# Batch 1's q transposed on TensorE instead of by DMA, and batch 2's loads requested ahead of the last w_out chunk

## The chip, the cores and the metric

The kernel runs on one core of a Trainium2 chip. A core has five engines with an instruction queue each: TensorE (PE, matrix products; its weight loads are listed apart as PEld), VectorE (DVE), ScalarE (ACT), GpSimd (POOL) and SyncE (SP, which here only requests transfers). Transfers are carried by 16 DMA engines; those that SP requests go through a queue that the profile calls q1, those that POOL requests through q0. The metric is the device time of one execution in microseconds (us); less is better. The kernel before took 294.74 us, the median of 3 runs (294.08 to 295.0).

## The reference: what is computed

An attention without a score matrix, followed by a two-layer block with a sine in it:

```
q_s = softmax of q over its 64 channels          # q, k, v: (8 batches, 8 heads, 576, 64), float32
k_s = softmax of k over its 576 positions
kv  = k_s^T v                                    # per batch and head, 64 x 64
x   = q_s kv, heads side by side                 # 4608 tokens x 512
h   = x @ w_in                                   # 512 -> 2048
g   = h + sin(alpha * h)^2 / (alpha + 1e-9)
out = g @ w_out                                  # 2048 -> 512, float32
```

## The kernel before, in words

Products are in bf16, sums in float32. Tokens are handled in 9 tiles of 512 for the two-layer block and in 8 batches of 576 for the attention, so a tile of the block needs one or two batches. The transposed attention output `xT`, `w_in` and `w_out` stay in on-chip memory. `w_out` comes in four chunks of 4 x 128 rows by `load_wout` (L110), requested by POOL because they are cast from float32 to bf16 on the way. q, k and v of a batch come by `load` (L94 in two halves, L96 in one piece), requested by SP into a pool of five staging buffers; `load_batch` requests all three.

The attention of a batch has these steps. `exp_q` and `exp_k` (ACT, L117) take exponentials. `norm_q` sums over the channels on DVE (L144, L145) and multiplies on POOL for the first half of the heads and on DVE for the second (L146), giving `qn`. `cast_v` (L131) makes v bf16 with a column of ones. q has to be transposed: `q_transpose_dma` (L196) does that by DMA from SP, `q_transpose` (L179 to L181) by products with an identity on PE into PSUM and a copy out. `kv_mm` (L157) forms the kv products and `kv_norm` (L167, L170) divides by the sums and writes `kbd`. `attn_chunk` (L214) multiplies `kbd` with transposed q, and a copy (L419 for batch 1) writes `xT`.

The order of the instructions on each engine is the order in which the program lists them; no scheduler changes it. Each engine takes its list in order and waits by semaphores. The products of one tile with `w_out` are a generator, and `take(os, n)` places the next n of them. For tile 0 that is `o_quad`: 64 products in four groups of 16, group c reading only chunk c of `w_out`. So the products from the 49th on need the fourth chunk, which `load_wout(3)` requests.

The stage at hand lies between tile 0 and tile 1 of the block. In it batch 1's attention is made, while the first 48 of the 64 products of tile 0 with `w_out` run on PE: 20, a short piece of attention for batch 0, then 26, then 2, then the kv products of batch 1, then 4 products, an attention pair for the first half of the heads, 2, the pair for the second half, 2 and the rest. Copies of the four finished sums (L260) and their stores (L263, eight of them on SP) follow. Tile 1's first products (L234) come next. PSUM tiles of this stage come from `ps_e`, two buffers with the tag "a" that are handed out in turn: `tp` of `q_transpose`, `kvp` of `kv_mm` and `xp` of the attention share them. The accumulators of `o_quad` are the four buffers of `ps_h`, which tile 1's products take over.

In the order written out, SP has, after v of batch 1: the two transposes of q of batch 1, the loads of batch 2, the eight stores, the loads of q and k of batch 3. POOL has `norm_q`'s first half and then the request of the fourth `w_out` chunk.

Of the kernel before, what the change touches and what calls it, by code (L numbers as in the profile page):

```python
# [23 lines left out]
def kernel(  # L24
# [51 lines left out]
    def src_view(t, b):  # L76
        return t[b].rearrange("(i e) (p j) d -> (e p) i (j d)", e=2, j=J)
# [7 lines left out]
    def load(name, t, b, halves=False, eng=nc.sync, gate=None):  # L85

        st = stage.tile([128, 4, J, D], F32, name=f"st_{name}", tag="st")
        for ii in range(2) if gate else ():
            gate(st[:, ii, 0, 0:1], zero)
        view = src_view(t, b)  # L90
        flat = st.rearrange("p i j d -> p i (j d)")
        if halves:
            for ii in range(2):
                eng.dma_start(out=flat[:, ii::2], in_=view[:, ii::2])  # L94
        else:
            eng.dma_start(out=flat, in_=view)  # L96
        staged[name, b] = st

    def load_batch(b):
        load("q", q, b)  # L100
        load("k", k, b)
        load("v", v, b)
# [6 lines left out]
    def load_wout(c):  # L109
        nc.gpsimd.dma_start(out=wout[:, 4 * c:4 * c + 4, :], in_=wout_v[:, 4 * c:4 * c + 4, :])  # L110
# [9 lines left out]
    def exp_q(b):  # L120
        A["qe", b] = att2.tile([128, J, 4 * D], BF16, name="qe")
        exp_to(A["qe", b], staged["q", b])

    def exp_k(b):
        A["ke", b] = att2.tile([128, J, 4 * D], BF16, name="ke")
        exp_to(A["ke", b], staged["k", b])

    def cast_v(b, engs):
        vv = vb[b % 2].rearrange("p j (i c) -> p i j c", i=4)
        for ii in range(2):  # L130
            engs[ii](vv[:, 2 * ii:2 * ii + 2, :, 0:D], staged["v", b][:, ii::2])  # L131

    def norm_q(b, engs):

        qe = A["qe", b].rearrange("p j (ii x d) -> p ii j x d", ii=2, x=2)
        A["qn", b] = qn = att1.tile([128, 2, J, 2 * D], BF16, name="qn")
        qs = small.tile([128, J, 4], F32, name="qs")
        if len(engs) == 1:
            nc.vector.tensor_reduce(qs, A["qe", b].rearrange("p j (i d) -> p j i d", i=4), axis=AXL.X, op=ALU.add)  # L139
            nc.vector.reciprocal(qs, qs)  # L140
        for ii in range(2):
            part = qs[:, :, 2 * ii:2 * ii + 2]
            if len(engs) == 2:
                nc.vector.tensor_reduce(part, qe[:, ii], axis=AXL.X, op=ALU.add)  # L144
                nc.vector.reciprocal(part, part)  # L145
            engs[ii % len(engs)].tensor_tensor(qn[:, ii].rearrange("p j (x d) -> p j x d", x=2), qe[:, ii],  # L146
                                               part.unsqueeze(3).to_broadcast([128, J, 2, D]), op=ALU.mult)
# [25 lines left out]
    def q_tile(b):  # L173
        if ("qT", b) not in A:
            A["qT", b] = att2.tile([128, 2, J, 128], BF16, name="qT")
        return A["qT", b]

    def q_transpose(b, ii, pool, eng):
        tp = pool.tile([128, 16, 128], BF16, name="tp", tag="a")  # L179
        q_transpose_ii(b, ii, 0, J, tp)  # L180
        eng(q_tile(b)[:, ii], tp[:, 0:J])  # L181

    def q_transpose_ii(b, ii, j0, j1, tp):

        for j in range(j0, j1):
            nc.tensor.transpose(tp[:, j - j0], A["qn", b][:, ii, j], identb)

    def q_transpose_dma(b, halves=False):
        for ii in range(2) if halves else (slice(0, 2),):
            out, in_ = q_tile(b)[:, ii], A["qn", b][:, ii]  # L190
            if not halves:
                out, in_ = out.rearrange("p ii j c -> p (ii j) c"), in_.rearrange("p ii j c -> p ii (j c)")
                in_ = in_.rearrange("p ii c -> p (ii c)")
            else:
                in_ = in_.rearrange("p j c -> p (j c)")
            nc.sync.dma_start(out=out, in_=in_, transpose=True)  # L196
# [14 lines left out]
    def attn_chunk(b, c, j0, j1, xp):  # L211

        ii, e = divmod(c, 2)
        nc.tensor.matmul(xp, kbd[b % 2][:, e, ii], A["qT", b][:, ii, j0:j1, e * 64:(e + 1) * 64],  # L214
                         start=True, stop=True)
# [6 lines left out]
    def mm_h(t, ni, wide=None, k0=0, k1=4):  # L222

        if ni == 0 and k0 == 0:
            G[t] = gpool.tile([128, nN, MF], BF16, name="g")
        if k0:
            hp = HP[t, ni]
        elif wide and ni % 6 in ((2, 3) if t == 0 else (4, 5)):
            hp = wide()
        else:  # L230
            hp = ps_h.tile([128, MF], F32, name="hp", tag="h")
        HP[t, ni] = hp
        for ki in range(k0, k1):
            nc.tensor.matmul(hp, win[:, ki, ni * 128:(ni + 1) * 128],  # L234
                             xT[:, ki, t * MF:(t + 1) * MF], start=(ki == 0), stop=(ki == 3))
        return hp
# [30 lines left out]
    ACT_CP, DVE_CP, GP_CP = nc.scalar.copy, nc.vector.tensor_copy, nc.gpsimd.tensor_copy  # L267
# [23 lines left out]
    ps_e = ES.enter_context(tc.tile_pool(name="ps_e", bufs=2, space=PSUM, reuse_waits="tile"))  # L291
# [54 lines left out]
    def h_slot(t, ni, sq, lag, wide=None):  # L346
        hp = mm_h(t, ni, wide, 2 if t < 2 and ni < 2 else 0)
        lag.append((t, ni, hp, sine(t, ni, hp, sq)))

    def flush(lag, keep):  # L350
        while len(lag) > keep:
            combine(*lag.pop(0))

    def o_quad(t, accs, engs):

        R = range(4)
        orders = [[(n, m) for p in (0, 2) for n in R for m in (p, p + 1)],
                  [(n, m) for n in R for m in R], [(n, m) for n in R for m in R],
                  [(n, m) for m in R for n in R]]
        for c in R:  # L360
            for n, m in orders[c]:
                mm_o(t, m, 4 * c + n, accs[m])
                if c == 3 and n == 3:
                    evac_o(t, m, accs[m], engs[m])
                yield

    def take(it, n=1000):
        for _ in range(n):
            if next(it, 0) == 0:
                return  # L370
# [4 lines left out]
    with ES:  # L375
        def lent():
            return ps_e.tile([128, 2, MF], F32, name="hh", tag="a")[:, 0]

        late = {6: lambda: load("q", q, 1, halves=True, gate=DVE_CP), 8: lambda: load_wout(2),
                13: lambda: load("k", k, 1, halves=True, gate=DVE_CP)}  # L380
        for ki in range(2):
            for ni in range(2):
                mm_h(0, ni, lent, ki, ki + 1)
        for ni in range(nN):
            h_slot(0, ni, "DPAPPAPPAPPAPPAP"[ni], lag, lent)
            flush(lag, 1)
            if ni in late:
                late[ni]()
        flush(lag, 0)

        accs = [ps_h.tile([128, dm], F32, name="hp", tag="h") for _ in range(4)]
        os = o_quad(0, accs, [DVE_CP, ACT_CP, DVE_CP, ACT_CP])
        take(os, 20)
        xp = ps_e.tile([128, 4, P], F32, name="xp", tag="a")
        for c in range(4):
            attn_chunk(0, c, 8, 9, xp[:, c])
        DVE_CP(xT[:, :, 8 * P:9 * P], xp)
        take(os, 26)
        exp_q(1)
        load("v", v, 1, halves=True)  # L400
        norm_q(1, [GP, V])
        load_wout(3)
        exp_k(1)
        cast_v(1, [ACT_CP, DVE_CP])
        q_transpose_dma(1, halves=True)
        load_batch(2)
        nc.scalar.activation(zero, zero, AX.Sin)
        take(os, 2)
        for ii in range(2):
            kv_mm(1, ii, ps_e, split=True)  # L410
            kv_norm(1, ii, ii + 1)
        take(os, 4)

        c0 = J * P
        for ii in range(2):
            xp = ps_e.tile([128, 2, 512], F32, name="xp", tag="a")[:, :, 0:7 * P]
            for e in range(2):
                attn_chunk(1, 2 * ii + e, 0, 7, xp[:, e])
            (ACT_CP, DVE_CP)[ii](xT[:, 2 * ii:2 * ii + 2, c0:c0 + 7 * P], xp)  # L419
            take(os, 2)  # L420
        take(os)
        load("q", q, 3)
        load("k", k, 3)

        for ki in range(2):
            for ni in range(2):
                mm_h(1, ni, lent, ki, ki + 1)
        for ni in range(nN):
            h_slot(1, ni, SQ[ni], lag, lent)
            flush(lag, 1)  # L430
        cast_v(2, [GP_CP, GP_CP])
        flush(lag, 0)
# [17 lines left out]
    os = o_stream(1)  # L450
# [54 lines left out]
    for t in range(3, nT):  # L505
        b = t + 1 if t + 1 < B else None
        os = o_stream(t - 1)
# [59 lines left out]
```

## Time and profile before

| | |
|---|---|
| median of 3 runs | 294.74 us |
| the profiled execution's own time | 295.0 us |
| its span, first to last instruction | 293.2 us |
| mean granted TensorE clock | 0.993 |
| PE busy | 275.7 us (94%) |
| ACT busy | 226.8 us (77%) |
| DVE busy | 188.0 us (64%) |
| POOL busy | 80.1 us (27%) |
| fourth `w_out` chunk: request to landing | 6.9 us, from 39.32 |
| the two transposes of q of batch 1: request to landing | 7.0 and 7.6 us |

The time given for an execution is a little longer than the span of its instructions. Times in the answers are us from the start of the span. A group of instructions is named by line, engine, operation, and what it writes and reads; "waited for" names what ended the idle time ahead of it. The chain of work that ended last is followed back from the last instruction through whatever released each step. The granted clock is that of TensorE, 1.00 being full. A DMA packet in the queues' counts is one contiguous piece of a transfer.

### The profile page before, as it was taken

The page shows a single profiled execution, that of the slowest core. Times are in us where ns is not written, and L with a number is a line of the kernel's source. Part 1 is how long each engine was busy: PE and PEld are TensorE (multiplying, and loading weights), DVE is VectorE, ACT ScalarE, POOL GpSimd, SP SyncE. Part 2 cuts the span into 40 slices and gives each one's busy share as a digit, 9 for nine tenths or more (in the row PEclk, how much of TensorE's full clock was granted, in tenths as well). Part 3 has the DMA queues.
Part 4 walks back from the last instruction along what each step waited for, and adds up shares of the span by engine and source line. Part 5 has one row for each costly group of instructions (what it writes and reads, how often), then busy time and mean ns, then how long its engine had stood idle before and what let it go on. Part 6 is the DMA issues. An engine that isn't in the chain of part 4 may idle for free.

```text
span 293.2 us, 4233 instructions
## 1 busy us (share of the span) xinstructions
PE 275.7 (94%) x1552; PEld 130.3 (44%) x1552; DVE 188.0 (64%) x279; ACT 226.8 (77%) x320; POOL 80.1 (27%) x74
## 2 busy tenths in 40 slices
PE   2799976999899999999999999999999999999995
PEld 1434442444445444444544454445444444444443
DVE  3867782599957847774767576766775455555412
ACT  4699862799748999889988998899887777777500
POOL 0678430466386646002420151005000000000000
PEclk9999997999999999999999999999999999999999
DMA  7999979993959986116941693115311111111142
GB/s 255 326 204 246 332 192 271 394 318 100 256 120 319 410 299 122 39 36 190 389 96 36 196 393 85 36 37 78 76 36 38 36 36 38 36 36 37 36 111 72
DMA packets 40261, 46.62 MB, mean 159 GB/s; under 512 B 18336, under 2 KB 23728, under 8 KB 40240
## 3 DMA queue, kind: packets, MB, share of 16 engines
q1 hardware_dynamic: 35760, 42.28, 48.1%
q0 software_dynamic: 4288, 3.93, 8.6%
q8 instruction: 12, 0.20, 0.3%
q10 hardware_dynamic: 192, 0.14, 0.2%
q14 instruction: 9, 0.07, 0.1%
HBM read 36.71 MB, written 9.44 MB: 157 GB/s over the span
## 4 chain that ended last, share of the span: by engine, by line
PE 82%; DMA 7%; DVE 3%; POOL 2%; issue 2%; SPq 1%; ACT 1%; POOLq 0%
PE hp L234 36%; PE op L254 33%; DMA st_w<-in_moe_w_in_dram 3%; PE hp L254 3%; PE hh L234 3%; DMA wout<-in_moe_w_out_dram 2%; PE kvp L157 2%; DMA qT<-qn 2%; PE xp L206 2%; DVE qs L144 1%; PE op L537 1%; PE op L234 1%; POOL s L244 1%; ACT s L240 1%; SPq L94 1%
## 5 line engine op out<-in xcount | busy, mean ns | idle before, releaser
L250 DVE SCALAR_TENSOR_TENSOR g<-s,inva_sb,hp 128x512 bf16<-128x512 f32 x130 | 96.2, 746 | 64.6 <-ACT s L242 54.2
L234 PE MATMUL hp<-xT,win 128*128 128x512 bf16 x520 | 129.9, 379 | 0.2 <-POOL win L321 0.2
L254 PE MATMUL op<-wout,g 128*128 128x512 bf16 x496 | 124.2, 379 | 0.0
L240 ACT ACTIVATE s<-hp,alpha_sb 128x512 f32<-128x512 f32 x130 | 87.7, 682 | 25.4 <-PE hp L234 24.2
L234 PEld LDWEIGHTS <-win 128*128 128x128 bf16 x576 | 56.2, 98 | 67.8 <-POOL win L321 0.9
L254 PEld LDWEIGHTS <-g 128*128 128x128 bf16 x560 | 54.5, 98 | 67.9 <-issue 7.4
L242 ACT ACTIVATE s<-s 128x512 f32<-128x512 f32 x112 | 70.5, 630 | 3.6
L146 POOL TENSOR_TENSOR qn<-qe,qs 128x1152 bf16<-128x1152 bf16 x12 | 25.3, 2128 | 72.3 <-DVE qs L140 62.4
L244 POOL TENSOR_TENSOR s<-s 128x512 f32<-128x512 f32 x29 | 30.5, 1063 | 27.1 <-ACT s L240 25.8
L260 DVE COPY o<-op 128x512 f32<-128x512 f32 (+2 forms) x33 | 22.1, 670 | 10.2 <-PE op L254 7.9
L117 ACT ACTIVATE qe<-st_q 128x1152 bf16<-128x1152 f32 x16 | 17.8, 1155 | 2.6 <-DMA st_q<-in_q_dram 2.5
L117 ACT ACTIVATE ke<-st_k 128x1152 bf16<-128x1152 f32 x16 | 17.9, 1151 | 2.5 <-DMA st_k<-in_k_dram 2.5
L254 PE MATMUL hp<-wout,g 128*128 128x512 bf16 x64 | 15.6, 397 | 4.0 <-DMA wout<-in_moe_w_out_dram 4.0
L139 DVE TENSOR_REDUCE qs<-qe 128x36 f32<-128x2304 bf16 x5 | 12.8, 2553 | 8.7 <-ACT qe L117 8.6
L131 POOL CAST vb<-st_v 128x1152 bf16<-128x1152 f32 x12 | 13.6, 1164 | 12.1 <-DMA st_v<-in_v_dram 7.9
L209 DVE CAST xT<-xp 128x512 bf16<-128x512 f32 (+1 forms) x18 | 13.4, 743 | 0.0
L157 PE MATMUL kvp<-vb,ke 64*128 64x130 bf16 x288 | 9.8, 216 | 0.8 <-ACT vb L310 0.8
L157 PEld LDWEIGHTS <-ke 64*128 64x128 bf16 x288 | 8.2, 93 | 4.1 <-issue 1.8
L117 ACT ACT_TABLE_LOAD x7 | 9.0, 1283 | 1.3 <-PEq L551 1.2
L234 PE MATMUL hh<-xT,win 128*128 128x512 bf16 x40 | 9.4, 379 | 0.0
L144 DVE TENSOR_REDUCE qs<-qe 128x18 f32<-128x1152 bf16 x6 | 8.0, 1330 | 1.9 <-ACT qe L117 1.9
L206 PE MATMUL xp<-qT,kbd 128*128 128x256 bf16 (+1 forms) x40 | 8.2, 286 | 0.4 <-DVE xT L209 0.3
(67 smaller groups left out, 114.6 us busy)
## 6 DMA issues: line engine op xcount, KB each, us to landing
out_dram<-o SPq DMA_DIRECT2D x70, 128.0 KB, 2.4
st_q<-in_q_dram SPq DMA_DIRECT2D x6, 1152.0 KB, 6.3
st_k<-in_k_dram SPq DMA_DIRECT2D x6, 1152.0 KB, 9.0
st_v<-in_v_dram SPq DMA_DIRECT2D x6, 1152.0 KB, 10.2
st_q<-in_q_dram SPq DMA_DIRECT2D x4, 576.0 KB, 5.4
st_k<-in_k_dram SPq DMA_DIRECT2D x4, 576.0 KB, 6.3
wout<-in_moe_w_out_dram POOLq DMA_DIRECT2D x4, 512.0 KB, 8.8
st_v<-in_v_dram SPq DMA_DIRECT2D x3, 576.0 KB, 8.0
```

Of the source, the lines that this page charges most:

```text
L117: nc.scalar.activation(dst[:, :, ii * 128:(ii + 1) * 128].rearrange("p j (x d) -> p x j d", x=2), src[:, ii::2], AX.Exp)
L131: engs[ii](vv[:, 2 * ii:2 * ii + 2, :, 0:D], staged["v", b][:, ii::2])
L146: engs[ii % len(engs)].tensor_tensor(qn[:, ii].rearrange("p j (x d) -> p j x d", x=2), qe[:, ii], part.unsqueeze(3).to_broadcast([128, J, ...
L157: nc.tensor.matmul(kvp[:, e, ii * 130:(ii + 1) * 130], ke[r, j, ii * 128:(ii + 1) * 128], vt[r, j, ii * 130:(ii + 1) * 130], start=(j == 0 ...
L206: nc.tensor.matmul(xp[:, e, 0:n], kt[:, e, ii], qT[:, ii, j0:j1, e * 64:(e + 1) * 64], start=True, stop=True)
L234: nc.tensor.matmul(hp, win[:, ki, ni * 128:(ni + 1) * 128], xT[:, ki, t * MF:(t + 1) * MF], start=(ki == 0), stop=(ki == 3))
L240: nc.scalar.activation(s, hp, AX.Sin, scale=alpha_sb[:, ni:ni + 1])
L242: nc.scalar.activation(s, s, AX.Square)
L244: nc.gpsimd.tensor_tensor(s, s, s, op=ALU.mult)
L250: nc.vector.scalar_tensor_tensor(G[t][:, ni], in0=s, scalar=inva_sb[:, ni:ni + 1], in1=hp, op0=ALU.mult, op1=ALU.add)
L254: nc.tensor.matmul(acc, G[t][:, ni, j * 128:(j + 1) * 128], wout[:, ni, :], start=(ni == 0), stop=(ni == nN - 1))
L260: eng(o[:, cols], acc)
```

## The change

Three lines of the stage between tile 0 and tile 1 change:

- `load_batch(2)` moves from behind the transposes of batch 1's q to directly behind the load of batch 1's v. On SP it is now ahead of everything but that load.
- The two DMA transposes of batch 1's q go. In their place each half of the heads is transposed on PE (9 products of 128 x 128 into a `ps_e` buffer) and copied out by DVE in one instruction of 1152 elements. In PE's order the 18 transposes stand ahead of the last two products with the third `w_out` chunk; in DVE's order the two copies stand between the cast of v and `kv_norm`.
- The four products with the fourth `w_out` chunk that stood directly behind the kv products go from there. All 16 products with that chunk now come behind the first attention pair.

```diff
         take(os, 26)
         exp_q(1)
         load("v", v, 1, halves=True)
+        load_batch(2)
         norm_q(1, [GP, V])
         load_wout(3)
         exp_k(1)
         cast_v(1, [ACT_CP, DVE_CP])
-        q_transpose_dma(1, halves=True)
-        load_batch(2)
+        for ii in range(2):
+            q_transpose(1, ii, ps_e, DVE_CP)
         nc.scalar.activation(zero, zero, AX.Sin)
         take(os, 2)
         for ii in range(2):
             kv_mm(1, ii, ps_e, split=True)
             kv_norm(1, ii, ii + 1)
-        take(os, 4)
```

POOL's list of instructions is the same in both kernels, and so is the place of `load_wout(3)` in it.

## The prediction

> **What bounds the kernel now.** I read the chain of work that ended last first: TensorE holds 82% of it, and the largest thing on it that is not TensorE between 20 and 70 us is one transfer. In order of time:
>
> ```profile
> 30.62 4.32 PE hp L254 x20
> ...
> 37.25 2.07 POOL qn L146
> 39.32 6.91 DMA wout<-in_moe_w_out_dram
> 46.23 0.04 issue
> 46.28 1.28 PE hp L254 x4
> 47.55 0.75 PE xp L214 x2
> 48.30 0.85 PE hp L254 x2
> 49.15 0.75 PE xp L214 x2
> 49.90 2.43 PE hp L254 x10
> 52.33 3.45 PE hp L234 x16
> ```
>
> Columns: start, length, what. The last chunk of w_out is requested at 39.32, lands at 46.23, and the 16 products that read it stand between it and the next stage. The waits of that stretch put 4.0 us on this landing:
>
> ```profile
> PE hp L254 <- DMA wout<-in_moe_w_out_dram: 4.0, 1, 4.0
> ```
>
> Then the busy time in stretches of 2 us. The last three columns are granted clock, DMA share, GB/s; the first two are the stretch and PE's busy time:
>
> ```profile
> 42.00:44.00 2.00, 0.28 (x10) 0.20 (x5) 1.31 (x5) 0.00 (x0) 0.00 (x0) 1.00 1.04 155
> 44.00:46.00 2.00, 0.00 (x0) 0.00 (x0) 0.00 (x0) 0.00 (x0) 0.00 (x0) 1.00 1.23 208
> 46.00:48.00 2.00, 1.72 (x6) 0.69 (x6) 0.41 (x1) 0.00 (x0) 0.00 (x0) 0.73 1.21 215
> 48.00:50.00 2.00, 2.00 (x6) 0.76 (x5) 0.34 (x2) 0.91 (x1) 0.00 (x0) 0.50 0.97 336
> ...
> 78.00:80.00 2.00, 0.83 (x4) 0.29 (x3) 1.97 (x2) 0.69 (x2) 0.88 (x1) 1.00 1.22 203
> ```
>
> After the idle 42.1 to 46.28 the clock is 0.50, from 46.9 to 50.3 in finer stretches. A gap of 1.65 us (78.5 to 80.2) costs no clock. Last, the DMA queues; q0 is what POOL requests (all weights that are cast), q1 what SP requests. Per queue: packets, MB, share of 16 engines. First pair 43 to 45 us (chunk 3 beside q's transposes), second pair 33.0 to 33.5 (chunk 2 beside k of batch 1), last line 35 to 38 (loads alone):
>
> ```profile
> q0 software_dynamic: 305, 0.31, 91.8%
> q1 hardware_dynamic: 307, 0.08, 29.7%
> ...
> q1 hardware_dynamic: 47, 0.11, 62.4%
> q0 software_dynamic: 51, 0.04, 54.7%
> ...
> q1 hardware_dynamic: 563, 1.22, 104.2%
> ```
>
> Where both queues have work they advance packet for packet, 305 to 307, although q1 alone ran at 450 to 500 packets per half us once q0 was empty (45.5 to 47).
>
> **The change part by part.** The stage is left when w_out's landing time T and the work behind it are over, so I compute the start of batch-tile 1's first product (L234), 52.17 now.
>
> *Removed: two DMA transposes on SP (L196).* They hold SP from 39.40 to 45.77 and feed only the two pairs of attention products (L214). Those wait for T now, since four w_out products stand ahead of them in PE's order. So removing them moves no wait on PE directly. It takes q1's transpose packets away from beside chunk 3.
>
> *Moved: the three loads of batch 2 (L96: q, k, v, 1.18 MB each).* SP issues them in 0.54, 0.49 and 0.46 us, now from 45.87. In the new order they follow v of batch 1, whose issue ends at 33.07: q and k go at about 33.1 and 33.7, v when the exponent of q of batch 1 frees its staging buffer (35.26). Nothing else stands on SP until the first stores behind T. On q1 they queue behind v of batch 1, whose packets end at about 39.3. 3.54 MB at 1.22 MB per 3 us is 8.7 us: q1 is full from 39.3 to about 48.0. Batch 2's data are first read after 68 us, so their earlier arrival is worth nothing. Loads q and k of batch 3 also go earlier, since the eighth store waits now for v of batch 2 (it lands at 47.04+11.6=58.6); no row shows a wait for them, so again nothing.
>
> *Added: 18 transposes on PE and two copies on DVE.* The rows are L186, 8 transposes in 0.75 us, hence 1.5 to 1.7 us for 18; 40.65 to about 42. They take the place of idle time. Each copy is 1152 elements out of PSUM: DVE's 896-element copy (L419) took 1.09 us, so 1.4 us (ACT's L326, 1024 elements in 0.99, gives 1.12 as the lower end). DVE's order is cast of v (ends 41.53), copy, copy, then the normalisation of kv: the copies end at 42.9 and 44.3. What is queued behind them: kv's first product group needs the first copy's PSUM buffer (43.0 to 43.6), the second group the second's (44.4 to 45.0); the normalisations (0.18+0.59 each now) end at 45.1 and 45.9; the first attention pair runs 45.15 to 45.7. All that was done at 43.4 is done at 45.9. Its cover is the wait for T; it costs nothing while T is over 45.7. At the lower end this is the floor: PE cannot be ready earlier than 45.7.
>
> *Moved: four w_out products behind the first attention pair.* The pair (0.37 us at full clock) leaves the path behind T; the number of products behind T stays 16.
>
> *The path behind T.* At full clock 16 products take 16 x 0.216 = 3.46 (the row of 20 in 4.32), and an attention pair 0.37. Now: 3.46 + 0.75 = 4.21, measured 46.28 to 52.17 = 5.89; the 1.68 left is half of the 3.4 us at clock 0.50. After: 3.46 + 0.37 = 3.83, plus what the clock takes, 0 to 1.68.
>
> *T, the unknown.* POOL's order is unchanged, so the request stays at 39.32. Chunk 3 is 528 packets on q0 (its count from 40.5 to 46). Beside transposes of 0.26 KB it took from 42.3 to the last half us before 46, and landed 0.4 later. Now its neighbours are packets of 2.3 KB. The row nearest to this is 33.0 to 33.5: 98 packets of both queues in 0.5 us; half of them gives 49, so 528 take 5.4 us. The start: the packets flowed 2.9 us after the request (42.25) with q1 idle, and 4.1 us after it for chunk 2 (26.01 to 30.1) with q1 loading. So T is 42.25+5.4+0.4 = 48.05 to 49.2; I take the middle, 48.6. Lower end: alone on the engines q0 moved 2297 packets in 11 us (16 to 27), so 528 take 2.5 us, T = 45.2, under the floor of 45.7. Upper end: chunk 3 waits until q1 is empty at 48.0, then 2.5 + 0.4, and up to 0.6 of stragglers: T = 50.9 to 51.5.
>
> *The sum.* L234 starts at 48.6 + 3.83 = 52.43, 0.26 later than now. PE would stand idle from 45.7 to 48.6, 2.9 us, midway between the gap that cost no clock (1.65) and the one that cost 1.68 (4.2). I take half, 0.85. Together +1.1 us. Everything behind 52 us is one dense chain to the end and moves with it. The profiled execution took 295.0 us outside for a span of 293.2, 0.26 above the median 294.74; 295.0+1.1 = 296.1 becomes **295.9** as a median.
>
> *Two rules of the Trainium skill against these rows.* The page "TensorE: Matmul & The Clock Gate", Part 1, has the array fall to half rate only after an idle window of about 3.4 us; the trace agrees with the slow time of 3.4 us here. By that rule a gap of 2.9 us might cost nothing, and the sum would be 295.0. The page "DMA: Bandwidth & Descriptors", Queues, rings and completion order, says that each engine switches between rings only at packet boundaries of some 9 to 17 descriptors; the counts 305 to 307 show one for one here, but with transposes. By that rule the loads could hold an engine for about a further us before each turn of chunk 3, and the sum would be about 297.
>
> **The rivals.**
>
> 1. *Chunk 3 is not slowed (faster).* One mechanism: q0 is served ahead of q1, or its slow start from 40.5 to 42.25 (39 packets) was due to the transposes and goes with them. For it: from 31.5 to 33 q0 got 271 packets and q1 33. Against it: q1 had hardly anything queued then, and 47 to 51 at 33.0 is an even split. T lies at 45.7 to 46.5, with little idle time, and L234 starts at 49.5 to 50.3: -2.6 to -1.8 us, 292.1 to 292.9. The forecast turns faster than before where T + 3.83 and the clock's loss come below 52.17.
> 2. *Chunk 3 waits for the whole backlog of q1 (much slower).* For it: chunk 2, requested at 26.01, moved no packet until 30.0, while q1 moved 344 packets from 28 to 30. Against: at 30.25 to 30.75 the two queues moved 48 and 48. T = 50.9 to 51.5 after 5 us of idle PE, so the full 1.68: L234 at 56.4 to 57.0, +4.2 to +4.8 us, 299.0 to 299.5. Without loss of clock 297.3 to 297.9.
> 3. *Nothing to be seen.* The loads are hidden in either place, T ends at 47.5 to 48.5, PE keeps its clock: -0.8 to +0.2 us, 293.9 to 294.9. It is the lower half of my own case.
>
> **How the numbers follow.** Even sharing (T 47.3 to 49.5, clock's loss 0 to 1.7: -1.0 to +2.9, 293.7 to 297.6), 0.55, rival 3 being part of it; rival 1, 0.20; rival 2, 0.25. 0.3%, 0.9 us, is about what a measurement of this kernel can tell from no change. Even sharing is slower by more in 0.29, within it in 0.20, faster in 0.06; rival 1 gives faster 0.16 and 0.04 within; rival 2 is all slower. Sum: faster 0.22, same 0.24, slower 0.54. The range goes from the middle of rival 1 to the middle of rival 2, 292.6 to 299.2, which leaves out a little under 2 in 10.
>
> **What would show it.** The landing of the fourth w_out transfer, 8.7 to 9.9 us after its request instead of 6.9; q0 and q1 with equal packet counts from about 43 to 48; two new copies of 1152 elements on DVE before 44.5, and an attention pair at about 45.2, ahead of the wait; PE idle about 3 us behind that pair, and a granted clock below 1.00 for up to 3.4 us after it; L234's 16 products starting at 52.4 to 53.3; from there every row the same, shifted. Wrong it would be with T under 47 or over 50, with a later landing of v of batch 1 (its cast is covered up to some 2.5 us only), or with another stage behind 52 us that lengthens or shortens.

## The result and the profile after

The changed kernel took 298.36 us (median of 4 runs, 298.07 to 298.68) against 294.87 us before (4 runs): a ratio of 1.0124, 95% interval 1.0102 to 1.0145. Measured again beside the last group of kernels below, the pair gave 298.19 and 294.54, ratio 1.012 (1.0058 to 1.0182). The forecast was 295.9 us in a range from 292.6 to 299.2: the direction and the range hold, but the loss is three times the predicted one (3.5 us for 1.2).

The profiled execution of the changed kernel took 298.07 us with a span of 296.3. Its chain of work in order of time (start, length, what):

```profile
37.26 2.07 POOL qn L146
39.33 11.31 DMA wout<-in_moe_w_out_dram
50.64 0.04 issue
50.69 1.01 PE hp L254 x2
51.70 0.75 PE xp L214 x2
52.44 4.17 PE hp L254 x14
56.61 3.45 PE hp L234 x16
```

The request of the last `w_out` chunk stands where it stood, at 39.33. It lands 11.31 us later instead of 6.91. The waits of the stretch put 6.4 us of idle PE on it (4.0 before):

```profile
PE hp L254 <- DMA wout<-in_moe_w_out_dram: 6.4, 1, 6.4
```

The two DMA queues over 44 to 49 us (packets, MB, share of 16 engines; q1 carries batch 2's loads, q0 the chunk):

```profile
q1 hardware_dynamic: 438, 0.97, 57.8%
q0 software_dynamic: 438, 0.45, 53.2%
```

Over these 5 us the two counts are equal, to the packet. The busy time by stretch (the first two columns are the stretch and PE; the last three granted clock, DMA share, GB/s):

```profile
44.00:46.00 2.00, 0.30 (x2) 0.05 (x1) 0.52 (x2) 0.91 (x1) 0.00 (x0) 1.00 1.13 287
46.00:48.00 2.00, 0.00 (x0) 0.00 (x0) 0.00 (x0) 0.00 (x0) 0.00 (x0) 0.95 1.10 284
48.00:50.00 2.00, 0.00 (x0) 0.00 (x0) 0.00 (x0) 0.00 (x0) 0.00 (x0) 0.50 1.09 336
50.00:52.00 2.00, 1.31 (x4) 0.53 (x4) 0.00 (x0) 0.00 (x0) 0.00 (x0) 0.50 0.48 186
52.00:54.00 2.00, 2.00 (x7) 0.66 (x6) 1.52 (x2) 0.00 (x0) 0.00 (x0) 0.50 0.00 0
54.00:56.00 2.00, 2.00 (x9) 0.83 (x8) 0.38 (x2) 0.58 (x1) 0.00 (x0) 0.84 0.28 63
```

PE was ready at 44.3, with nothing but the chunk to wait for, and the work behind the landing then ran at half clock until 54.6. From the landing to tile 1's first product (L234, at 56.45) it took 5.8 us, where the same work is 3.83 us at full clock.

### The profile page after: what moved, and what is told of

Its sections match the earlier page's. It is cut to its first block, busy times and chain, and to the rows that moved or that the text cites. A ratio compares the mean times of both kernels' runs of the same rounds, so it can differ in the third digit from the quotient of the medians.

```text
span 296.3 us, 4263 instructions
## 1 busy us (share of the span) xinstructions
PE 277.6 (94%) x1570; PEld 131.6 (44%) x1570; DVE 189.0 (64%) x281; ACT 226.8 (77%) x320; POOL 79.8 (27%) x74
## 4 chain that ended last, share of the span: by engine, by line
PE 81%; DMA 9%; DVE 3%; POOL 2%; issue 2%; SPq 1%; ACT 1%; POOLq 0%
PE hp L234 36%; PE op L254 32%; DMA wout<-in_moe_w_out_dram 4%; DMA st_w<-in_moe_w_in_dram 3%; PE hp L254 3%; PE hh L234 3%; PE kvp L157 2%; PE xp L206 2%; DMA qT<-qn 1%; DVE qs L144 1%; PE op L537 1%; PE op L234 1%; POOL s L244 1%; ACT s L240 1%; POOL qn L146 1%
## 5 line engine op out<-in xcount | busy, mean ns | idle before, releaser
L234 PE MATMUL hp<-xT,win 128*128 128x512 bf16 x520 | 129.9, 379 | 0.2 <-POOL win L321 0.2
L234 PEld LDWEIGHTS <-win 128*128 128x128 bf16 x576 | 56.2, 98 | 67.8 <-POOL win L321 0.9
L254 PEld LDWEIGHTS <-g 128*128 128x128 bf16 x560 | 54.6, 98 | 69.5 <-issue 9.5
L254 PE MATMUL hp<-wout,g 128*128 128x512 bf16 x64 | 16.2, 408 | 6.4 <-DMA wout<-in_moe_w_out_dram 6.4
L234 PE MATMUL hh<-xT,win 128*128 128x512 bf16 x40 | 9.4, 379 | 0.0
L260 ACT COPY o<-hp 128x512 f32<-128x512 f32 x2 | 1.2, 585 | 10.8 <-PE hp L254 10.8
```

What stands on the lines that cost most here:

```text
L234: nc.tensor.matmul(hp, win[:, ki, ni * 128:(ni + 1) * 128], xT[:, ki, t * MF:(t + 1) * MF], start=(ki == 0), stop=(ki == 3))
L254: nc.tensor.matmul(acc, G[t][:, ni, j * 128:(j + 1) * 128], wout[:, ni, :], start=(ni == 0), stop=(ni == nN - 1))
L260: eng(o[:, cols], acc)
```

## The experiments

The theory: batch 2's loads, released early, share the DMA engines with the last `w_out` chunk packet for packet; the chunk lands late, and the clock granted to PE falls while it waits. The rivals: the chunk is slow for a reason of its own; transposing on PE or the new order of products costs the time. Two groups of four kernels were measured, each group on one chip with the kernel before beside it (median 295.31 in the first, 294.54 in the second; the changed kernel and the kernel before again belong to the second).

**Loads held back.** Batch 2's loads wait for a one-element copy on DVE behind kv's normalisation. The rest is the changed kernel.

```diff
-        load_batch(2)
         ...
         for ii in range(2):
             kv_mm(1, ii, ps_e, split=True)
             kv_norm(1, ii, ii + 1)
+        load("q", q, 2, gate=DVE_CP)
+        load("k", k, 2)
+        load("v", v, 2)
```

> The changed kernel with one edit: batch 2's loads wait for a 1-element copy on DVE behind kv's normalisation (44.5 us), so that they are not in the queue while the fourth w_out chunk is transferred. Theory A (the chunk shares the DMA engines packet for packet with those loads): its packets flow from about 42.3 us and finish 2.5 us later, it lands at 45.2 to 46, tile 1's first product starts at 49 to 50 instead of 56.45, the clock stays at 1.00 or nearly so, and the time is 291.5 to 293.5 us, below both kernels. Theory B (the chunk is slow by itself, as it was requested late and q0 starts slowly): it still lands near 48 to 50 us, and the time is 295.5 to 298.

Measured: 290.30 us, ratio to before 0.9832 (0.9777 to 0.9888). It beats both kernels, and lies 1.2 us under the range that I expected. The chain:

```profile
38.23 5.90 DMA wout<-in_moe_w_out_dram
44.12 0.04 issue
44.17 0.38 PE hp L254
44.54 0.05 issue
44.60 0.54 PE xp L214 x2
45.14 3.02 PE hp L254 x14
48.16 3.45 PE hp L234 x16
```

and q0 from 41.5 to 43 us, with q1 empty:

```profile
q0 software_dynamic: 305, 0.31, 124.7%
```

Alone the chunk moves 305 packets in 1.5 us, beside the loads 438 in 5 us. It lands 5.90 us after its request, the clock stays at 1.00, and L234 starts 3.9 us after the landing (47.99), close to the 3.83 worked out. The theory that the chunk is slow by itself falls. (This profile reached the stage 1.1 us earlier, because its first 16 us, which no edit touches, were shorter; that is about what the time lies under my range. So I compare distances from the chunk's request. From there to L234 it is 12.85 us before, 17.12 changed, 9.76 here.)

**Loads moved alone.** The kernel before, with only the loads ahead of the DMA transposes on SP.

```diff
         load("v", v, 1, halves=True)
+        load_batch(2)
         norm_q(1, [GP, V])
         ...
         q_transpose_dma(1, halves=True)
-        load_batch(2)
```

> The kernel before with only the loads of batch 2 moved ahead of the two DMA transposes on SP; transposes stay on the DMA and the products in their old order. Theory A: the chunk is delayed as in the changed kernel, landing at 50 to 51 us, and the transposes, behind 3.5 MB on the same queue, land after it, at 53 to 55; the time is 299 to 303 us, above the changed kernel's 298.4. Theory C (what costs the time is transposing on PE and the new order of the products, not the loads): the time stays within 1 us of before, 294 to 296.

Measured: 301.07 us, ratio 1.0187 (1.0117 to 1.0257). The chunk lands 10.5 us after its request, and behind it q's transposes are late too, since they now queue behind 3.5 MB. The waits of the stretch:

```profile
PE hp L254 <- DMA wout<-in_moe_w_out_dram: 7.5, 1, 7.5
PE xp L214 <- DMA qT<-qn: 2.0, 1, 2.0
```

Moving the loads does the harm by itself, as the theory had it (landing at 50 to 51, 299 to 303 us); transposing on PE takes some of it back.

**One load early.** As with the loads held, but q of batch 2, a third of the bytes, is requested early again.

```diff
         load("v", v, 1, halves=True)
+        load("q", q, 2)
         ...
-        load("q", q, 2, gate=DVE_CP)
-        load("k", k, 2)
+        load("k", k, 2, gate=DVE_CP)
         load("v", v, 2)
```

> As with all of batch 2's loads held, but q of batch 2 (1.18 MB, a third of them) is requested early again, behind v of batch 1; k and v stay held. Theory A, packets shared one for one: q's packets fill q1 from about 39 to 42 us, the chunk's flow from 41 to 42.3 us on; beside at most one us of q's they finish in 2.5 to 3.5 us, it lands 6 to 7.5 us after its request (held: 5.9; changed kernel: 11.3), and the time is 290.3 to 292. A theory in which any load ahead in q1 delays the chunk's start by the full four us and more gives 8 us or more and 292.5 or more.

Measured: 292.42 us, ratio 0.9921 (0.9888 to 0.9953); the chunk lands 7.6 us after its request. The time to landing grows with what is ahead in q1: 5.9, 7.6, 11.3 us with none, one and three of the loads. Even sharing explains only a part of the 1.7 us between the first two: from 42 to 44 us the chunk already had 376 of 400 packets, and its last 30 then took from 44.5 to nearly 46, with nothing on q1 until 45.5. Why they straggle was not followed. The landing is a tenth above the range that I gave, the time 0.4 us. The time has another cause, which this profile shows:

```profile
44.50:45.00 0.50, 0.00 (x0) 0.00 (x0) 0.24 (x3) 0.50 (x1) 0.00 (x0) 1.00 0.16 27
45.00:45.50 0.50, 0.00 (x0) 0.00 (x0) 0.00 (x0) 0.23 (x1) 0.00 (x0) 1.00 0.14 23
45.50:46.00 0.50, 0.01 (x1) 0.00 (x1) 0.00 (x0) 0.00 (x0) 0.00 (x0) 1.00 0.46 36
...
47.00:47.50 0.50, 0.50 (x3) 0.15 (x1) 0.43 (x1) 0.00 (x0) 0.00 (x0) 0.50 0.97 373
49.50:50.00 0.50, 0.50 (x3) 0.19 (x2) 0.00 (x0) 0.37 (x1) 0.00 (x0) 0.50 1.06 415
```

PE idled for only 1.7 us, and the clock still fell to 0.50 for some 3.4 us. Only this run has a trace. Of the ten runs, five have a mean clock of 0.994 (292.71 to 294.15 us, mean 293.4) and five of 1.000 (290.79 to 292.12, mean 291.4). So the drop, about 1.9 us, comes in some runs and not in others; how long PE idled in the nine without a trace is not known.

**PE kept busy.** The changed kernel, with products of no use in the wait; their result is overwritten.

```diff
+        nxt = None
         for ii in range(2):
-            xp = ps_e.tile([128, 2, 512], F32, name="xp", tag="a")[:, :, 0:7 * P]
+            xp = nxt if nxt is not None else ps_e.tile([128, 2, 512], F32, name="xp", tag="a")[:, :, 0:7 * P]
             for e in range(2):
                 attn_chunk(1, 2 * ii + e, 0, 7, xp[:, e])
+            if ii == 0:
+                nxt = ps_e.tile([128, 2, 512], F32, name="xp", tag="a")[:, :, 0:7 * P]
+                for _ in range(28):
+                    nc.tensor.matmul(nxt[:, 0], identb, win[:, 0, 0:7 * P], start=True, stop=True)
```

> The changed kernel with 28 products of 448 columns on PE, whose result is overwritten, between the first attention pair and the wait for the chunk; nothing is left out. The chunk's landing should not move (50.6 us). If the lower clock behind the wait costs what the rows say (1.9 us of the 5.8 from the landing to tile 1's first product), the granted clock stays at 1.00, the product starts at 54.5 to 54.8 us instead of 56.45, and the time falls by 1.5 to 2 us to 296.3 to 297. If the products behind the wait are slow for another reason, the time stays at 298.4.

Measured: 295.70 us (10 runs), ratio to before 1.0004 (0.9968 to 1.004), a little under the 296.3 to 297 expected. The chunk lands as late as ever, 11.5 us after its request, but the clock stays at 1.00. In the timeline (start, length, engine and line), the filling products and what follows:

```profile
44.65 5.47 PE L423 MATMUL xp<-win,identb 128*128 128x448 bf16 x28 [0.29 <-DVE kbd L170]
49.96 0.38 PE L254 MATMUL hp<-wout,g 128*128 128x512 bf16 x1
50.39 0.54 PE L214 MATMUL xp<-qT,kbd 128*128 128x448 bf16 x2
50.77 3.19 PE L254 MATMUL hp<-wout,g 128*128 128x512 bf16 x14
53.79 3.62 PE L234 MATMUL hp<-xT,win 128*128 128x512 bf16 x16
```

53.79 lies 3.83 us behind 49.96, the full-clock sum. Against the changed kernel the time is 2.5 to 2.7 us less, where the clock explains 1.9; in this profile the rest is the shorter start, which was not followed into the other runs.

**The changed kernel and the kernel before again**, the first on the same chip as the last group of kernels, the second for another profile.

> The changed kernel as it is, beside the others on one chip. Landing of the chunk 11 to 11.5 us after its request, time 297.5 to 299. It serves as the measure for the run with PE kept busy (295.7): the difference should be 1.5 to 2 us by the clock alone; if it stays near 2.7, a part of that came from the first 16 us of the execution, which were 1 us shorter in that profile.

> The kernel before as it is, for a second profile. If the 1.2 us that the changed kernel makes good behind 60 us is a property of the two kernels, batch 2's transposed q lands again about 4.9 us after the copy that precedes it on the chain, against 3.9 in the changed kernel; if it is chance, the two are alike here.

Measured: 298.19 us and a landing 11.7 us after the request for the changed kernel, a little over the 11 to 11.5 expected; 295.94 us (one run) and 6.8 us for the kernel before. The latter's transposes of batch 2 stand on the chain with 4.43 us, the former's with 3.84: the same order as in the first profiles (4.87 and 3.94), with a smaller difference.

These two profiles also show that the clock's loss is not one fixed amount. Two rows of the changed kernel, then two of the kernel before:

```profile
46.00:48.00 2.00, 0.00 (x0) 0.00 (x0) 0.00 (x0) 0.39 (x1) 0.00 (x0) 0.72 1.13 293
54.00:56.00 2.00, 2.00 (x7) 0.64 (x5) 0.89 (x2) 0.24 (x1) 0.00 (x0) 0.50 0.00 0
...
44.00:46.00 2.00, 0.00 (x0) 0.00 (x0) 0.00 (x0) 0.00 (x0) 0.00 (x0) 0.69 1.18 197
50.00:52.00 2.00, 2.00 (x8) 0.70 (x7) 1.09 (x1) 0.59 (x1) 0.00 (x0) 0.61 0.99 385
```

In the changed kernel the clock is at 0.50 from 46.9 to 57.1 (in its first profile from 47.8 to 54.6), and from the first product after the landing (51.41) to L234 (58.03) it takes 6.62 us, 2.8 more than at full clock. In the kernel before it is at 0.50 from 44.7 to 51.6, and the same path takes 6.82 us, 2.6 more than at full clock, where the first profile had 1.68.

**Held, in the old order of products.** As with the loads held, and `take(os, 4)` back behind the kv products.

```diff
         load("v", v, 2)
+        take(os, 4)
```

> As with all of batch 2's loads held, and the four w_out products again directly behind the kv products, as in the kernel before. If the order of the products is worth what the rows say (one attention pair of 0.37 us that then stands behind the landing), tile 1's first product starts 0.3 to 0.8 us later relative to the chunk's request (9.76 us after it when held), and the time is 290.6 to 291.3. If the order carries more of the gain, the time is over 292.

Measured: 290.36 us, ratio 0.9872 (0.9807 to 0.9938), against 290.30 with the new order, on another chip: no difference that these runs can tell. From the request to L234 it is 9.93 us, 0.17 more, where I had expected 0.3 to 0.8. This kernel differs from the one before almost only in that q is transposed on PE: its loads are issued from 44.37, there from 45.87. So transposing on PE alone is worth about 4.2 us (294.54 to 290.36). Between the two profiles the spans differ by 4.7 us: 2.9 from the chunk's request to L234, 1.25 behind L234, and 0.5 in the start of the execution, which no edit touches. The chunk lands 5.7 us after its request rather than 6.8 to 6.9, with no transpose packets beside it, and PE's gap of 1.56 us cost no clock in this profile.

**The chunk requested first.** The changed kernel with POOL's request ahead of `norm_q`.

```diff
-        norm_q(1, [GP, V])
         load_wout(3)
+        norm_q(1, [GP, V])
```

> The changed kernel with the request of the fourth w_out chunk ahead of batch 1's normalisation on POOL, so at about 33 us instead of 39.3. Theory A: its packets flow from about 37 us, packet for packet beside v of batch 1, and finish about 6 us later; it lands at 43 to 45; v of batch 1 is delayed by up to 2.5 us to 43, and kv with it, so PE is ready at 46 to 47; tile 1's first product starts at 50 to 51, and the time is 292 to 294.5 us. Theory D (the delay of v costs more than the chunk gains): 296 us or more.

Measured: 293.68 us (10 runs), ratio 0.9945 (0.9913 to 0.9976). Now v of batch 1 pays, as expected. The queues over 37 to 42 us, and v's cast on ACT and DVE, which stood at 39.10 and 40.59:

```profile
q1 hardware_dynamic: 462, 0.99, 57.9%
q0 software_dynamic: 461, 0.47, 55.2%
...
41.77 1.17 ACT L131 CAST vb<-st_v 128x1152 bf16<-128x1152 f32 x1 [1.78 <-DMA st_v<-in_v_dram]
...
43.61 0.77 DVE L131 CAST vb<-st_v 128x1152 bf16<-128x1152 f32 x1 [3.58 <-DMA st_v<-in_v_dram]
```

PE idles 3.6 us for v instead of 6.4 for the chunk, and L234 starts at 52.46, some 2 us later than I had expected; about 1.5 of it is the clock, which fell here too (0.55 from 48 to 50).

## Why the prediction was right, and what was mis-sized

The mechanism was right: the loads become ready at once, they share q1 and q0 evenly with the chunk, and the chunk's landing sets the end of the stage. With distances from the chunk's request or from its landing, term by term:

- *Start of the chunk's packets.* Predicted 42.25 to 43.4, with the middle taken. They flowed from 43.5. The row with loads beside it (chunk 2, 4.1 us after its request) was the right one, not the middle: 0.7 us. Alone they flowed 2.8 us after the request.
- *The rate.* Predicted 49 packets in half a microsecond; 438 in 5 us are 44: another 0.6 us. The half microsecond from 33.0 that I took had both queues busy only for a moment; a longer row would have been safer.
- *The end.* I added 0.4 us for the receipt. The last 41 packets of the chunk dribbled from 49 to 50.5, and the landing was at 50.64: 0.7 us more than at the steady rate. Why they lag stays open. In all T was 50.64 for 48.6.
- *The clock.* Predicted a loss of 0.85, half of 1.68, with 1.68 as the most; in the first profile it was 1.93, in the second 2.8. The low clock comes in steps (3.41 us in the kernel before, 6.83 and 10.24 in the two profiles of the changed kernel), and what is lost is half of the part in which PE works. So the half was a mean over outcomes and no likely value, and 1.68 was no upper bound. "A gap of 1.65 us costs no clock" was wrong as a lower bound: in the profile with one load early a gap of 1.7 us cost it, in the one in the old order a gap of 1.56 us did not. What beside the gap's length decides (where it falls, or how busy PE is around it) was not tested.
- *Two copies on DVE.* Predicted 1.4 us each from a copy of float32; the two together took 1.42 us. From a bf16 PSUM tile DVE reads about twice as fast (1152 elements in 0.71 us, against 896 of float32 in 1.09). It changed nothing, PE being ready at 44.3 instead of 45.7, the floor that I had named, and still waiting for the chunk. With the loads held it matters: there PE is ready 0.2 us before the landing.
- *The transposes removed* were costed at nothing, beyond rival 1, which had them as one reason for the chunk's slow start. With the loads held back the chunk lands 5.7 to 5.9 us after its request instead of 6.8 to 6.9: the transposes beside it had cost it about a microsecond. In the changed kernel the early loads buried that gain.
- *"Everything behind 52 us moves with it"* was wrong by 1.2 us in our favour. L234 starts 4.28 us later, yet the span is only 3.1 longer. The difference is made good by batch 2's transposes: the one on the chain lands 29.06 us after L234 in the kernel before and 27.75 in the changed one. All seven profiles of kernels that transpose batch 1 on PE have 3.77 to 4.02 us there, the three others 4.32 to 4.87; v of batch 3, ahead of these transposes in q1, is requested 0.75 us sooner after the store before it begins. That store's second half takes SP 1.35 us in those three and 0.6 in the others; why stays open.

So 1.1 predicted, plus 2.04 for the landing, 1.08 for the clock, less 1.2 further on, gives 3.0; the spans differ by 3.1. Of the rivals, the one where the chunk isn't slowed is excluded by equal packet counts in three kernels, and the one where it waits for the whole backlog as well, although the late start and the lagging end brought T near its lower bound and L234 (56.45) into its range.

That the range holds is partly luck. Even sharing, the case that came true, was given 293.7 to 297.6 us, with T up to 49.5, and two of the signs named for being wrong came: T over 50, and a stage behind 52 us that shortens. The range reached to 299.2 only because the backlog rival was given weight; and without the 1.2 us made good further on, which nobody foresaw, the time would have been about 299.6, outside it.

By parts, from the medians: transposing on PE -4.2 us, the order of the products nothing that can be told, the early loads +7.9 (298.19 to 290.30, on two chips). Not all of that arises in the stage. From the chunk's request to L234 the early loads cost 7.4 us (9.76 to 17.12), and transposing on PE gains 2.9 (12.85 to 9.93). The profiles of the held kernels also begin the stage 0.5 and 1.1 us sooner, by a shorter start of the execution whose cause stays open.

One thing the diff hides: on SP both the move of `load_batch(2)` and the loss of the transposes ahead of it release the loads. Had it stayed at its old place in the program, nothing but v of batch 1 would have stood ahead of it on SP, so by the program's order it would have been issued just as early; no run shows this.

## What to carry to other kernels

A transfer that stands in a queue behind a slow instruction may be well placed by accident: whoever removes the instruction must put something in its place that holds the transfer back, here one DVE copy of one element per staged half. When a critical transfer and a load that is not urgent overlap on two queues, count on equal packet counts and on a late start and a ragged end too. And when PE waits, price the clock as a chance of nothing or of one or more steps of 3.41 us, not as a share.

## What the runs showed of the hardware that was not expected

- Two queues with plain rows (2.2 and 1.0 KB a packet by the profile's counts) get equal numbers of packets over 5 us: 438 to 438, 462 to 461, and with the loads moved alone 455 to 450 (43.5 to 48.5). The page "DMA: Bandwidth & Descriptors" of the Trainium skill, Queues, rings and completion order, speaks of turns of some 9 to 17 descriptors; equal counts over 5 us don't tell the length of a turn, but the shares are even.
- In the seven traces in which the clock fell in this stage, it stood at 0.50 for one, two or three times 3.41 us: 3.41 (before, one load early, chunk first), 6.83 (changed, before again), 10.24 (loads moved alone, changed again). The kernel before varies with it: of its 19 runs beside the first group, nine have a mean clock of 0.992 to 0.994 and take 294.6 us in the mean, ten have 0.987 or 0.988 and take 296.3.
- The clock fell after 1.7 us of idle PE in the run with one load early that has a trace, and in five of the ten runs by their mean clock. The page "TensorE: Matmul & The Clock Gate", Part 1, asks for an idle window of about 3.4 us in a window that runs freely. That it falls or not from run to run fits a free window; that so short a gap is enough differs from the rule, and the measurement decides.
- DVE copies 1152 bf16 elements per partition out of PSUM in 0.71 us; 896 float32 elements took it 1.09 us.
